# Level rows of the first batch picked on TensorE, and a state product with unequal weight widths, in a GateLoop and PReLU kernel

## The chip, the cores and the metric

The kernel runs on one core of one Trainium2 chip. It is one launch, and the time is that of the whole launch on the device in microseconds (us), inputs read from HBM and the output written to HBM. Below, PE is TensorE, DVE is VectorE, ACT is ScalarE, POOL is GpSimd, and SP is SyncE, whose queue issues every DMA of this kernel.

## The reference

Two blocks follow each other, all in float32. The first is a recurrence with a complex, data-dependent gate (4 batches, 8 heads, 768 tokens, head dimension 48):

```
mag = sqrt(a_re^2 + a_im^2);  scale = min(mag, 0.999) / (mag + 1e-6)
a = (a_re + i a_im) * scale
for t:  S = a[:, :, t, :, None] * S + k[t] v[t]^T      # S is complex, 48 x 48 per head
        y[t] = q[t] @ real(S)
```

Its output, as 3072 rows of 384, goes through the second block:

```
h = x @ w_in                                  # 3072 x 2048
g = max(h, 0) + alpha * min(h, 0)
out = g @ w_out                               # 3072 x 384
```

## The kernel before

**Units.** The tokens of a batch are cut into 6 chunks of 128, so there are 24 units u = 6b + c, and six of them make the first batch. Real and imaginary parts lie on neighbouring partitions: 96 partitions are 48 dimensions times two. `gates` makes the decays and phases of up to three chunks at a time with DVE and ACT and sends them through HBM; `loads` brings q, k, phases (`PP`) and decays (`T`) of a unit back in.

**Inside a unit** (function `unit`). Each half of 64 tokens is split in six levels h = 1, 2, 4, 8, 16, 32: at level h, a run of h keys meets the run of h queries after it. DVE brings keys and queries to a common point (L579, L581, L637), ACT copies them together (L660, L676), PE multiplies them (`ps_lv`, L596), and DVE or ACT masks the result into `A` (L620, L610). The output of the level then needs the rows of v that belong to the level's keys, in their order, on partitions 0 to 63 of each half: that is the tile `VL`, six levels wide, and the matmuls are those of L760 into `ps_y`.

**The rows of v.** `loads_v` loads the chunk of v as it is (`V`, L523 to L528) and `VL` besides. For h = 1, 2 and 32, `VL` comes straight from HBM in ten DMAs a unit (L547); for h = 4, 8 and 16 `half_rows` first copies the rows of a whole batch from HBM to HBM in the wanted order (`vsc`, six DMAs a batch, L480), and two DMAs a unit fetch them (L551). `V` and `VL` each have one buffer.

**The state.** Keys are transposed on PE (`ps_kt`, L708), and ACT copies the result into `T`: 96 columns at L710, and once more the first 32 of them into columns 96 to 127 at L711, to fill the weights up. The state products (`ps_kv`, L720) are, for each of 8 heads, a first half and a second half of 64 weight columns, for one or two halves of tokens: 32 matmuls of 64 rows by 64 weight columns with 48 moving columns (16 in the last chunk of a batch, which needs one half only). DVE adds them to the state (L728, L731), and L746 multiplies state and queries into `ps_y`. ACT copies `ps_y` out (L771) and it goes to HBM as the next block's input.

**The second block.** 256 tokens make an m. `features` and `two_features` compute h (`ps_h`, L817 and L839) and the gate; `outputs` computes the first 512 rows with plain products (`ps_o`, L867), and from then on `seven` makes four half-size blocks of the output from seven products (L957). The weights come in eight pieces of each matrix and are put together from halves of 64-bit words by ACT and DVE (`to_f32`, L435 to L445) into `w_in_sb` and `w_out_sb`.

**The order.** Every function above is a generator, one per stream of work, and the string `ORDER` says whose turn it is: each letter runs one generator to its next `yield`, which issues a few instructions. Engines run their own queue in that order and wait for each other by semaphores; the numbers in the `yield`s are not read when the kernel is built. Letters A to I are the gates, J the loads, K `half_rows`, L `loads_v`, M to O the weights, P to Z and a to m the 24 units, n the loads of x, o the second block.

A float32 matmul of the program is two matmul instructions on PE, each with its own load of weights, so the profile counts twice as many as the code. The shape of PE's array that a matmul asks for follows from its rows and weight columns: 128x32 at L596, 128x64 at L746, 64x64 at L720 and L760, 128x128 for the second block.

Of the kernel before, what the change touches and what calls it, by code (L numbers as in the profile page):

```python
# [30 lines left out]
    "ABMABAAABABAAAAAAABMAAAAAMAAAABABBBJMMNMAAAJABBAAKAAAKJJAAAAAAAABBBABJABBBBBBNMBNPBBBPNPJBJKJKJBJBBB"  # L31
    "PNBBBPBBBBBBBBBPPPOOOOJLJCPJJLLKKCPOJLLLMLLLLLLLMLLJJOPOPOPNOPPPPONNPPQCPPPQNQCCCCPPPPPPPPPPQQPQPCNC"
    "CCPPPPPPPPPCQQNCCCCCONCCCQOQCNPCPQQQOJMMJPPLMLLJCNQQNORCJLnLCMLLJJJLCCCLLLLQCQRCRQQCCOQNQQQoooooooLL"
    "LNQQRRQNooQQCCCCCNCooQoOoQRQoCQORCCNRRoNooooooORoQOMJONQQoooooRNNOOQQQQRQQROQOQDQQJLRLLnLJJORoLLoooo"
    "LLDMLRNNoLLLLLLooooJDooDDRoooSoSoRRRRRRRRooooooooDRRoRRoRooooRNNNRDSDoDRoDRDSOooooooooRoDoDRSSRJJJJR"
    "RSNSSRRRRDoooooDSDTOooODSLRRoSSoLMLLMJLJLLLLLooSoDSoOTSNoooooSNoOooSSoSoSNSSSSoSDooToSoSooSTSNoooOOo"
    "oNMLLLLLTTSoTSTDSOoTTSDoooooDoDSOKTNoNNNOSSSTSSTSJJJMJLSDDoooooSoooooDJLSSLoOToNTToooToOoOOoooooTTOT"
    "TToTDDTToooooUTnTTooLLLJJLJLDLLLUooooTDToDDoooLLLoLKDoJJJToTTUooDDoDDDTDJTDDDoooooUoTTUTUTTUUUUoVooo"
    "oooooUoTUUVUTTTTVooooooooUUUEJJLLLJJELLLLLLLLLJoLLooooVoEooooUUoUUUEoEVooooooEoEoUVUoUUUoooooUooooEU"
    "UVVUUVUVVVEEEooooooooVoUoKEUVKVUUUUJKKEUUUUKJJJVEVVooVooooEoooEEooEooVVVooooVVVVVVoWoWooooooVoVooJLL"  # L40
    "LJnWooVooVWoLLLLVWWEVEVEEEWEVWWLLLLLLLLEVWWVJEJoKJoooooooooooVVVWVWVVVELKVVLLLLJLJJLLLJJWoWWEWoooooo"
    "oooXXooEEEoEEoooooooooooooooooWWWWWWWoooWXoEWLLLoEoooooooooooWWooooWWoooXoXWWEEEWEEWoJLLLJoooWXWWWEW"
    "XWWWXYWXLWWLLFYXJLnLJJLoooooooXooooooooooooooXXXXXXoooooFoooooooXXFXXoXXXoXooooooooXoXoXYYooooLLLLLL"
    "LLooXXYYXooXYXYYLYooooXooooXFYFooooooXXXXYXYXFYoFYXXXLXLJLJJJLJLLLFooooooooYYoJooooooooooFoooooYYYFF"
    "YooYYooYYoJJLLLJLLJLoZoYooZooYooooFFoooFoYooYYFZoooFFLLooooooooooZooooZZYZYZYFZZYFYFYoooFZYYYZYZYYFo"
    "YooFFYooooooooooFFLLYJJJLooZooooooZZoooooooooooLnFLLFLJLLLJFooLJLLLLZaaFooooooZZoooZFaoFFZZoooooooaF"
    "FoZZZoZFFFoooooooZoooZooaaoooZoZoZZaaZFFFooFJJaoaaZooooooooooooZZZaZZZaZZaoooooooZaoaooabooooooooooo"
    "oooaaooabbZLLZLGJJLLJLJLLGLLLLLaaaoaaooaGooaoooooooJoboaoooaGoobGabaaaJJabbaLKKKoGbGoooooooooooobbbo"
    "ooGGooooGGooooboooooooooababaaGbaGGbGabaLaooooooooocoobLLJJGnKLoooooooooLoLLooobbooocbLLLLLJbbGGGoob"
    "ocooooooLLLKboboboooGGoboooocboooooobbccboocbGbGooooooocccGGoobboooobbbbooooooooooooGcGGKJGGGobcbcbo"  # L50
    "ocbJLJbbLLLJJLocccoooooooooooGooooccGcccocccGdGcoooooooooooocococoocooccoooGGGGcJLLLLLLLLLLdGcocGcoo"
    "oooooodoodooocccddcJJJcdcooooooooooooooooddLLccLHLcJJJLLLJLLdoLdHLLnoooooooodKLLLdddoddooooooooooooo"
    "ooddodddddooHeddoooeodooooodedoHdoooooooooooededdddeeoHddHooooooooeHeeoooHoooddoooooooooooooooddoeee"
    "oddoKJJJJddLLLJeJLLLJJJJLLLeoeoooooooooeHooooHooooooooooffHHooooeeeLJJLLLLLooooooHHHHHHHfooeeooeeeeo"
    "oooooeeoooooooooeoeoooeeeoeHHHfoHeHgefeoooooeeefeHeeKHooofofeeoJJHffoooooooonofHLJLLLLLLLHHooooooooo"
    "offfgoLLJLJJJLLLoofffooooooogHoLooooffoofHHfooooHHHoooooooooofffffoofoofoogoHooooHooooffooooofHHfffH"
    "ffHohhogooooooffgffgffofofhfgogooooooooooooooooggIJJLLLLLLLLJJJIJJgLLLLLLggIgoggIooooooIooooooooooog"
    "goghgIoggogoghIoogooooooogooIoogoogoghhgIhgghIhgoIooohhoooooooooioooooooohogIoIoghggghghhgIggLLLLJJn"
    "hhoooooooooooiLLLLLJLLLLLLJJooohhIhIhhIoooohhhIIihooooooooihoooooooooooooiIhooooooooooooooooooohhJoo"
    "oiiiihhohihIIIohihoooooooJhhihhihihLoohIIiooooooooooiihooooooooooooooiioihILLLoooIiiiijJJLLLJJLLLJji"  # L60
    "iJLLLLLIoiooiooiIiooioiIjiioIIIIIoIooooooooooIIIoiIoooooojiijijiijJIojjjjoooooooooooooooooooijjjjiio"
    "oiijJnJJJLLLLJLLojooooooooooooooooojjjjjjjkkjooooooooojjooojookooooooojoojoookookjkoooookkoooooooooo"
    "oojJJLLLLLLLLLjjoooooookoooooooooojookoooooookooojjjjkjkjjjkLjjkooooooooolkkoLLJJJJJooooookkkokkkook"
    "kooookokkooooolloookooklkllkkkkkloooollooooooooooolJLLLLLLLLLLJLLooooooooooloooooooooklkklkkkklkkLLL"
    "LLnlllooLLLJJLLooooooooooooooollolllloolllooooooolooolmmolloLLLLLoooooloooololmmlooooooooooolooooooo"
    "olmlmlmomomooooooooomoooooooooomoooolmlmlmooooomLLLLLLmomoooooooooLLLLoooooommoooommllmmmmmllLLLLooo"
    "oommoooooomooomooommmmmmmmmomooooooooooommmoooooooooooonoooooooooooooooooooooooooooooooooooooooooooo"
    "oooooooooooooooooooooooooooooooooooooooooooooooooooooooooooooooooooooooooooooooooooooooooooooooooooo"
    "oooooooooooooooooooooooooooooooooooooooooooooooooooooooooooooooooooooooooooooooooooooooooooooooo")
# [28 lines left out]
def kernel(  # L98
# [99 lines left out]
    def step(*args, **kwargs):  # L198
# [5 lines left out]
        KQ=3, PP=1, T=2, V=1, WQ=2, W=1, St=3, xT=2, raw0=1, raw1=1, raw2=1, raw3=1, g0=6, g1=6, g2=6, ot=2, top=2,  # L204
# [245 lines left out]
    def piece(dst, *key):  # L450
        if words:
            return (yield from to_f32(dst, *key))
        t = yield ACT(2 * DM, ("raw", *key))
        nc.scalar.copy(dst, raws[key])
        del raws[key]
        raw_done(*key, t)
        return t
# [10 lines left out]
    def half_rows():  # L468

        one = NCH * D2  # L470
        for b in range(B):
# [44 lines left out]

    def loads_v():
        for u in range(NU):
            b, c = divmod(u, NCH)
            yield DMA(172, ("KQ", u), takes=(R["V"],))  # L520
            L = loaded[u]
            L["V"] = V = work.tile([P, HP, D2], F32, tag="V", name="V", bufs=1)
# [31 lines left out]
            L["Vp"] = {name: VL[:, i] for i, name in enumerate(LEVELS)}  # L554
# [8 lines left out]
    def unit(u):  # L563
# [140 lines left out]
        for i in range(2):  # L704
            e = yield PE(0.333, k_, takes=(R["misc"],), n=2)
            t = ps.tile([P, HP, D2], F32, tag="misc", name="ps_kt")
            for p in range(4):
                nc.tensor.transpose(t[:, p], KQ[:, 1, 4 * i + p], ident[:D2, :D2])  # L708
            e = yield ACT(HP * P + 80, e, ("decays", u))
            nc.scalar.copy(T[:, 4 * i:4 * (i + 1), 0:D2], t)  # L710
            nc.scalar.copy(T[:, 4 * i:4 * (i + 1), D2:P], t[:, :, 0:P - D2])  # L711
            R["misc"].put(e)
# [3 lines left out]
        for n in range(H):  # L716
            for j in range(0, P, HC):
                for s in range(1 if last else 2):
                    rows = slice(HC * s, HC * (s + 1))
                    nc.tensor.matmul(kv[s][j:j + HC, n], lhsT=T[rows, n, j:j + HC],  # L720
# [422 lines left out]
```

## Time and profile before

| | |
|---|---|
| time, three runs | 762.88 us median (760.21 to 762.91) |
| the profiled execution | 765.08 us, of which the span of instructions is 763.4 us |
| PE busy | 674.9 us, 11728 matmul instructions |
| DVE busy | 605.4 us |
| ACT busy | 487.6 us |
| DMA | 130.61 MB, mean 171 GB/s |
| TensorE clock granted | full in nearly the whole span |

The busy share is told by stretch below. A matmul instruction is counted as busy from its start to the end of its way through the array, so neighbours overlap: a PE that is 100% busy may still have room between the starts of its matmuls. In timelines the first column is the start, and the distance from start to start is what a group of matmuls costs; the second column, its length, includes the way of the last one through the array.

### The profile page before, as it was taken

Reading aid. Unit: us, or ns where it says so; the run is one execution under the profiler, and the core shown is the slowest. Engines: PE = TensorE matmul, PEld = TensorE weight load, DVE = VectorE, ACT = ScalarE, POOL = GpSimd, SP = SyncE. Lnnn points to the kernel's source line nnn. Section 1 sums busy time; section 2 is a strip of 40 time slices with the busy share of each in tenths; the row PEclk is TensorE's granted clock in tenths of the full one; section 3 lists DMA queues with packets and bytes.
Section 4 is the critical chain, followed back from the end, with each engine's and each line's share of the span. In section 5 each row is a group of like instructions: output and inputs, shape, how many; then the busy total and the mean of one; then the engine's idle time right before and its main releaser. Section 6 shows DMA issues by size and latency. Waiting matters only on the chain.

```text
span 763.4 us, 26774 instructions
## 1 busy us (share of the span) xinstructions
PE 674.9 (88%) x11728; PEld 581.2 (76%) x11728; DVE 605.4 (79%) x798; ACT 487.6 (64%) x886; POOL 13.1 (2%) x48
## 2 busy tenths in 40 slices
PE   0024578999999999999999999999999999999998
PEld 0024456776767888888888889888888988889987
DVE  7889889998999799898986898888996765742323
ACT  8868888985658576946693666756584544453330
POOL 5000000000000000000000000000000000000000
PEclk9999999999999999999999999999999999999999
DMA  9999989979677936787668854865745743421000
GB/s 257 273 258 230 267 236 274 232 216 245 192 194 201 254 83 140 210 223 187 177 170 210 234 123 102 227 188 135 185 129 171 183 104 81 112 43 53 1 21 21
DMA packets 177180, 130.61 MB, mean 171 GB/s; under 512 B 66280, under 2 KB 168424, under 8 KB 176616
## 3 DMA queue, kind: packets, MB, share of 16 engines
q1 hardware_dynamic: 177064, 128.91, 64.3%
q8 instruction: 92, 1.51, 0.9%
q14 instruction: 24, 0.20, 0.1%
HBM read 100.52 MB, written 35.42 MB: 178 GB/s over the span
## 4 chain that ended last, share of the span: by engine, by line
PE 53%; DMA 16%; DVE 11%; SPq 6%; ACT 4%; issue 2%; DVEq 0%; ACTq 0%
PE ps_h L839 19%; PE ps_o L957 17%; PE ps_lv L596 4%; PE ps_y L760 3%; DVE KQ L637 3%; DMA PP<-phs 3%; PE ps_o L867 3%; DMA T<-decs 2%; PE ps_kv L720 2%; SPq L547 2%; PE ps_y L746 2%; DMA xT<-ysc 2%; DMA shared<-in_w_out_dram 2%; DMA VL<-vsc 2%; PE ps_h L817 1%
## 5 line engine op out<-in xcount | busy, mean ns | idle before, releaser
L839 PE MATMUL ps_h<-xT,w_in_sb 128*128 128x256 f32 x960 | 228.6, 384 | 0.7 <-DVE shared L854 0.6
L839 PEld LDWEIGHTS ps_h<-xT,w_in_sb 128*128 128x128 f32 x960 | 176.9, 190 | 22.6 <-DVE shared L854 0.8
L637 DVE TENSOR_TENSOR KQ<-KQ,T 96x1024 f32<-96x1024 f32 x120 | 145.8, 1215 | 28.6 <-PE ps_lv L596 18.9
L957 PE MATMUL ps_o<-w_out_sb,shared 128*128 128x192 f32 x624 | 111.4, 329 | 0.8 <-ACT top L973 0.4
L854 DVE TENSOR_TENSOR shared<-shared,ps_h 128x512 f32<-128x512 f32 x80 | 54.5, 682 | 68.2 <-ACT shared L852 67.9
L957 PEld LDWEIGHTS ps_o<-w_out_sb,shared 128*128 128x128 f32 x624 | 102.4, 190 | 3.5 <-DVE top L963 0.8
L848 ACT ACTIVATE shared<-ps_h 128x512 f32<-128x512 f32 x80 | 47.7, 596 | 80.6 <-PE ps_h L839 80.2
L957 PE MATMUL ps_o<-shared 128*128 128x192 f32 x448 | 80.3, 331 | 0.7 <-DVE top L963 0.7
L852 ACT ACTIVATE shared<-shared,al 128x256 f32<-128x256 f32 x160 | 74.5, 505 | 1.9
L957 PEld LDWEIGHTS ps_o<-shared 128*128 128x128 f32 x448 | 72.7, 190 | 3.3 <-DVE top L963 1.4
L660 ACT COPY WQ<-KQ 96x1024 f32<-96x1024 f32 x48 | 49.9, 1039 | 33.9 <-DVE KQ L637 33.7
L596 PE MATMUL ps_lv<-WQ 96*32 96x32 f32 x2304 | 34.4, 203 | 38.2 <-DVE WQ L579 26.0
L596 PEld LDWEIGHTS ps_lv<-WQ 96*32 96x32 f32 x2304 | 26.2, 116 | 52.4 <-DVE WQ L579 26.0
L817 PE MATMUL ps_h<-xT,w_in_sb 128*128 128x256 f32 (+1 forms) x240 | 53.3, 357 | 4.5 <-DMA xT<-ysc 4.5
L867 PE MATMUL ps_o<-w_out_sb,shared 128*128 128x384 f32 x128 | 51.3, 509 | 5.6 <-DVE shared L826 4.2
L817 PEld LDWEIGHTS ps_h<-xT,w_in_sb 128*128 128x128 f32 x240 | 41.9, 203 | 16.4 <-DMA xT<-ysc 5.2
L760 PE MATMUL ps_y<-A,VL 64*48 64x64 f32 x2304 | 49.1, 225 | 4.5 <-DMA VL<-vsc 4.4
L610 ACT ACTIVATE A<-ps_lv,columns 128x64 f32<-128x64 f32 x144 | 38.3, 334 | 21.4 <-PE ps_lv L596 21.0
L771 ACT COPY T<-ps_y 48x512 f32<-48x512 f32 x48 | 27.7, 576 | 34.5 <-PE ps_y L760 33.7
L676 ACT COPY W<-KQ 96x512 f32<-96x512 f32 x48 | 30.6, 637 | 29.5 <-DVE KQ L637 29.5
L760 PEld LDWEIGHTS ps_y<-A,VL 64*48 64x48 f32 x2304 | 39.4, 123 | 11.0 <-DMA VL<-vsc 5.8
L596 PE MATMUL ps_lv<-KQ,W 96*32 96x32 f32 x1536 | 23.4, 203 | 15.9 <-ACT W L676 15.8
(108 smaller groups left out, 955.8 us busy)
## 6 DMA issues: line engine op xcount, KB each, us to landing
T<-decs SPq DMA_DIRECT2D x48, 384.0 KB
PP<-phs SPq DMA_DIRECT2D x24, 387.0 KB
KQ<-in_q_dram SPq DMA_DIRECT2D x48, 192.0 KB
phs<-gate SPq DMA_DIRECT2D x14, 577.5 KB
decs<-gate SPq DMA_DIRECT2D x7, 1152.0 KB
KQ<-in_k_dram SPq DMA_DIRECT2D x40, 192.0 KB
vsc<-in_v_dram SPq DMA_DIRECT2D x24, 288.0 KB
VL<-vsc SPq DMA_DIRECT2D x48, 144.0 KB
```

The source lines that it names most:

```text
L596: nc.tensor.matmul(t[64 * i + j:64 * i + j + HC // 2, p], lhsT=keys(n, g), rhs=queries(n, g), start=True, stop=True)
L610: nc.scalar.activation(a[:, :, cols], t[:, :, at:at + name], AF.Copy, scale=s)
L637: nc.vector.tensor_tensor(out=x, in0=x if x0 is None else x0, in1=m, op=ALU.mult)
L660: nc.scalar.copy(z.rearrange("p i n t -> p i (n t)").rearrange("p i (m h) -> p m i h", h=h), bass.AP(tensor=KQ.tensor, offset=KQ.offset + ...
L760: nc.tensor.matmul(o, lhsT=Vp[h][64 * i:64 * i + 64, s, e_ * D:(e_ + 1) * D], rhs=a, start=False, stop=(s == 1 and h == LEVELS[-1]))
L817: nc.tensor.matmul(p, lhsT=w_in_sb[:, f // 2, kk, f % 2 * P:(f % 2 + 1) * P], rhs=x_of[m][:, kk, c * P:(c + n) * P], start=(kk == 0), stop ...
L839: nc.tensor.matmul(p[:, i], lhsT=w_in_sb[:, f // 2, kk, i * P:(i + 1) * P], rhs=x_of[m][:, kk], start=(kk == 0), stop=(kk == NK - 1))
L848: nc.scalar.activation(gt, p, AF.Relu, scale=-1.0)
L852: nc.scalar.activation(some_, some_, AF.Copy, scale=al_1[:, f + i:f + i + 1])
L854: nc.vector.tensor_tensor(out=gt, in0=gt, in1=p, op=ALU.add)
L867: nc.tensor.matmul(sums[0], lhsT=gt, rhs=w_out_sb[:, f], start=(f == start), stop=(f == stop))
L957: nc.tensor.matmul(z, lhsT=a[:, i], rhs=w[:, i], start=i == 0, stop=i == F2 - 1)
```

## The change

1. In the first batch, `VL` isn't loaded any more. A new generator `picks` (letter p) makes it on PE: a matrix of zeros and ones per level (`pick`, cut out of the identity by six copies on POOL) times `V` gives the rows of the level. For each of the six units these are 12 matmuls of 128 rows by 64 weight columns with 192 moving columns, four to a PSUM buffer of the ring `lv`, and three copies by ACT of 128x384 from PSUM to `VL`. The 12 `VL` DMAs of each of these units and the six `vsc` DMAs of the batch are gone. The other three batches do as before.
2. `V` has a second buffer for the even units of the first batch. It lies in the place of row block 14 of `w_out_sb`, and the picking matrices lie in that of row block 15, so the last piece of `w_out` is put together only after the last pick and after unit 4.
3. The second half of the state product has 32 weight columns in place of 64, in every unit: 64 and 32 columns make the 96 rows of the state. ACT's second copy (L711) is gone. The number of matmuls stays.
4. `ORDER` is another string altogether, found anew with longer transfers assumed.

The diff without the strings of the order:

```
-        KQ=3, PP=1, T=2, V=1, WQ=2, W=1, St=3, xT=2, raw0=1, raw1=1, raw2=1, raw3=1, g0=6, g1=6, g2=6, ot=2, top=2,
+        KQ=3, PP=1, T=2, V=1, Va=1, VL=1, WQ=2, W=1, St=3, xT=2, raw0=1, raw1=1, raw2=1, raw3=1, g0=6, g1=6, g2=6, ot=2, top=2,
...
     def to_f32(dst, *key):
         n = 2 * DM
-        ta = yield ACT(n + 100, ("raw", *key), takes=(R["top"],))
+        picked = [("picked", 0), ("V free", NCH - 2)] * (key == ("out", NF // 2 - 1))
+        ta = yield ACT(n + 100, ("raw", *key), *picked, takes=(R["top"],))
...
     def half_rows():
-        for b in range(B):
+        for b in range(1, B):
...
+    def v_ring(u):
+        return "Va" if u < NCH and u % 2 == 0 else "V"
+
     def loads_v():
         for u in range(NU):
             b, c = divmod(u, NCH)
-            yield DMA(172, ("KQ", u), takes=(R["V"],))
+            yield DMA(172, ("KQ", u), takes=(R[v_ring(u)],))
             L = loaded[u]
-            L["V"] = V = work.tile([P, HP, D2], F32, tag="V", name="V", bufs=1)
+            if v_ring(u) == "V":
+                V = work.tile([P, HP, D2], F32, tag="V", name="V", bufs=1)
+            else:
+                V = w_out_sb[:, NF - 2].rearrange("p (n e) -> p n e", n=HP)
+            L["V"] = V
...
             done["values", u] = t_
-            yield DMA(98)
+            if not b:
+                done["VL", u] = t_
+                continue
+            yield DMA(98, takes=(R["VL"],))
...
             del vsc_of[u]
-            L["Vp"] = {name: VL[:, i] for i, name in enumerate(LEVELS)}
+            done["V", u] = t
...
+    pick = w_out_sb[:, NF - 1].rearrange("p (l t) -> p l t", l=len(LEVELS))
+    for k, h in enumerate(LEVELS):
+        nc.gpsimd.tensor_copy(pick[:, k].rearrange("p (m h) -> p m h", h=h), halves(ident, h)[:, :, 0])
+
+    def picks():
+        for u in range(NCH):
+            n = P - (u + 1 == NCH)
+            for at in range(0, len(LEVELS), 2):
+                e = yield PE(0.7, ("VL", u), takes=(R["lv"],), mode=2, n=4)
+                L = loaded[u]
+                p = ps.tile([P, 2, 2, D2], F32, tag="lv", name="ps_vl", bufs=2)
+                for k in range(2):
+                    for i in range(2):
+                        nc.tensor.matmul(p[HC * i:HC * (i + 1), k], lhsT=pick[0:n, at + k], rhs=L["V"][0:n, 2 * i:2 * i + 2],
+                                         start=True, stop=True)
+                if u + 1 == NCH and at + 2 == len(LEVELS):
+                    done["picked", 0] = e
+                t = yield ACT(4 * D2, e, takes=() if at else (R["VL"],))
+                if not at:
+                    VL = work.tile([P, len(LEVELS), 2, D2], F32, tag="VL", name="VL", bufs=1)
+                    L["Vp"] = {name: VL[:, i] for i, name in enumerate(LEVELS)}
+                nc.scalar.copy(VL[:, at:at + 2], p)
+                R["lv"].put(t)
             done["V", u] = t
...
             nc.scalar.copy(T[:, 4 * i:4 * (i + 1), 0:D2], t)
-            nc.scalar.copy(T[:, 4 * i:4 * (i + 1), D2:P], t[:, :, 0:P - D2])
             R["misc"].put(e)
...
         for n in range(H):
-            for j in range(0, P, HC):
+            for cols in (slice(0, HC), slice(HC, D2)):
                 for s in range(1 if last else 2):
                     rows = slice(HC * s, HC * (s + 1))
-                    nc.tensor.matmul(kv[s][j:j + HC, n], lhsT=T[rows, n, j:j + HC],
+                    nc.tensor.matmul(kv[s][cols, n], lhsT=T[rows, n, cols],
                                      rhs=V[rows, n // 2, (n % 2) * D:(n % 2 + 1) * D], start=True, stop=True)
...
-        for name in ("V", 1, 4, 16, 32):
+        for name in (v_ring(u), "VL", 1, 4, 16, 32):
             R[name].put(e)
+        done["V free", u] = e
...
+        plan.add(picks())
         plan.run(ORDER)
```

More of the change, by code (lines that the diff above doesn't have):

```diff
@@ L36 @@
[L36 to L50, printed above, removed]
```

66 lines of the change are left out of this document (41 added, 25 removed).

## The prediction

> **What bounds the kernel.** I read the busy time by stretches first, then PE's timeline, then the waits and the chain. Stretches (start and end, length, then busy time and instructions of PE, PE's weight loads, DVE, ACT, POOL, then clock, DMA share, GB/s):
>
> ```profile
> 80.00:100.00 20.00, 14.84 (x387) 12.41 (x378) 17.02 (x29) 17.96 (x32) 0.00 (x0) 1.00 1.01 273
> 160.00:180.00 20.00, 20.00 (x381) 15.08 (x380) 17.07 (x28) 12.36 (x23) 0.00 (x0) 1.00 0.89 244
> 200.00:240.00 40.00, 39.04 (x725) 28.64 (x722) 38.12 (x44) 27.73 (x47) 0.11 (x1) 1.00 0.73 194
> 280.00:320.00 40.00, 40.00 (x624) 35.88 (x623) 37.39 (x45) 30.05 (x51) 0.11 (x1) 1.00 0.67 166
> 500.00:550.00 50.00, 49.43 (x860) 44.10 (x854) 42.18 (x50) 33.29 (x66) 0.14 (x2) 1.00 0.63 161
> ```
>
> Up to about 140 us DMA (0.9 to 1.0) and DVE share the limit and PE has gaps (77 us up to 140). From there PE is full: between 240 and 700 us its stretches leave 4.6 us idle in all. PE runs in order, so after 220 us whatever lengthens its row of matmuls lengthens the kernel.
>
> The second view is PE's timeline late in the kernel, where nothing is waited for. The distance from start to start is the cost:
>
> ```profile
> 640.40 0.46 PE L596 MATMUL ps_lv<-WQ 96*32 96x32 f32 x32
> 640.79 0.93 PE L760 MATMUL ps_y<-A,VL 64*48 64x64 f32 x48
> ...
> 647.81 0.46 PE L596 MATMUL ps_lv<-WQ 96*32 96x32 f32 x32
> 648.08 0.49 PE L596 MATMUL ps_lv<-KQ 96*32 96x32 f32 x32
> 648.50 0.70 PE L839 MATMUL ps_h<-xT,w_in_sb 128*128 128x256 f32 x2
> ...
> 655.13 1.15 PE L720 MATMUL ps_kv<-V,T 64*64 64x48 f32 x64
> 656.21 0.70 PE L839 MATMUL ps_h<-xT,w_in_sb 128*128 128x256 f32 x2
> ...
> 662.03 0.65 PE L746 MATMUL ps_y<-KQ,St 96*48 96x64 f32 x16
> 662.61 0.46 PE L596 MATMUL ps_lv<-WQ 96*32 96x32 f32 x32
> ...
> 686.46 1.14 PE L720 MATMUL ps_kv<-V,T 64*64 64x48 f32 x32
> 687.52 1.38 PE L746 MATMUL ps_y<-KQ,St 96*48 96x64 f32 x32
> ```
>
> Two things are to be seen. First, a change of array shape costs time: 32 matmuls of L596 take 0.27 us when the same shape follows (647.81 to 648.08), 0.39 and 0.42 when another follows (640.40, 648.08). So a change is worth 0.12 to 0.15 us; I take 0.13. It is paid where only the width changes too: from L746 (128x64) to L596 (128x32), 16 matmuls take 0.58 us, eight rounds of two side by side at 0.056 and one change. Second, matmuls on separate parts of the array run side by side, and time goes by rounds: L720 takes 1.08 us for 64 matmuls and 1.06 for 32 (last chunk of a batch, half of the rows). That is 16 rounds of 0.059 and one change. A round of 32 weight columns is 0.27 / 8 = 0.034.
>
> **The change part by part.** I sum against the profiled execution, 765.1 us (span 763.4 and 1.7 around it), 2.2 above the median of 762.9.
>
> *State products, all 24 units.* The order of matmuls is now, per head, 64 wide for one or two token halves, then 32 wide, and so on: shapes 64x64 and 64x32 alternate 15 times in a unit. In the two programs' orders I count 288 changes of shape before and 681 after, 360 of them inside state products. A head then costs two rounds of 64 (0.118), a change (0.13), two rounds of 32 (0.068), a change (0.13): 0.446 us, 3.57 a unit against 1.08, so +2.5. Lower end: the widths still share their rounds and only changes are paid at the cheapest, 15 x 0.12 = 1.8. If a change between these two isn't one, zero (first rival). The value taken is nearest to the rows of L746 and L596, which differ in width alone. In the timeline 17 units have their product after 220 us: 42.5, of which 3 go into PE's 4.6 us idle: +39.5. Four units lie between 140 and 220 (10 us, 3 in gaps): +7. Three lie before 120 us, in PE's gaps: +1; without that cover 7.5. Sum +47.5.
>
> [...]
>
> *First batch's DMAs.* Gone are 6 x 576 KB of `VL` (eight of 24 KB, two of 48, two of 144) and 6 x 288 KB of `vsc`, 5.2 MB. At the 253 to 279 GB/s of the first 100 us that is 20 us of all DMA engines, and 78 of 700 issues on SP, which took about 0.6 us each. The chain shows where that tells: DMA and SP carry most of it between 74 and 126 us (w_in, w_out, phases, decays, gates, and ten issues in SP's queue), and pieces at 167 to 178 and 204 to 214.
>
> ```profile
> PE 53%; DMA 16%; DVE 11%; SPq 6%; ACT 4%; issue 2%; DVEq 0%; ACTq 0%
> ```
>
> What comes after is DVE, whose idle time between 20 and 240 us is 18.4 us in all, and DVE has as much work for the first batch as before. So at most 18 us, at least none; I take -10, about the middle, since the chain between 126 and 165 us is DVE and PE already. V's second buffer belongs here: its load waits no longer for the last matmul of the unit before.
>
> *Picks.* 72 matmuls, 144 instructions of 192 columns. L957 has that width: 16 in 2.60 us, 0.163 each. Two column halves side by side, as in L746, give 72 x 0.163 = 11.7 us; one after the other 23.4. Units 0 to 3 lie where PE has gaps; units 4 and 5 (24 matmuls, 3.9 us) don't: +4. Ends: 0 and 23. Outside the state products, changes of shape grow by 40 in the first batch (13 of them in units 4 and 5, 1.7 us) and fall by 7 later (0.9): +1.
>
> *ACT.* L711 is gone:
>
> ```profile
> L711 ACT COPY T<-ps_kt 128x128 f32<-128x128 f32 x48 | 13.4, 279 | 0.0
> ```
>
> ACT isn't the limit; what counts is that PE's weight loads waited for it 7.5 us at L708 and 3.3 at L720, 6.7 of that before 220 us. I take -2, ends -10.8 and 0. The 18 copies of picks are nearest to L710 (128x384 from PSUM, 0.479): 8.6 us, less 12 x 0.279 in the same batch, +5 us of ACT. ACT's gaps up to 240 us hide it (12.4 of 20 busy at 160); without them +5.
>
> *New waits, costed at nothing.* The first copy of a unit's picks waits on ACT until `VL` is free, that is for the last L760 of the unit before; behind it stand masks, gates and weights. ACT waits for the same event to copy `ps_y` (L771), so it waits once. The last piece of `w_out` waits for the last pick; behind it stand two ACT steps of 1.0 and 1.1 us and one of DVE of 0.95, and the 23rd `ps_o` group of 384 columns follows closely: up to 3 us of PE if the cover, two groups of the second block, isn't there. Six POOL copies (0.32 each for the nearest, 64x64) come ahead of the masks, while PE's first matmul waits until 26 us.
>
> Sum: 47.5 - 10 + 4 + 1 - 2 = +40.5. The profiled execution would be 806 us, the median 803.
>
> **The rivals.**
>
> *The two widths don't count as a change* (20%). All changes of shape in the trace go between parts of the array that overlap; 64 columns at 0 and 32 columns at 64 don't. If PE runs them side by side as before, the state products cost nothing and the rest, -10 + 4 + 1 - 2 = -7, makes it faster: 756 us. For it: narrow weights are quick (a round of 0.034 against 0.059). Against it: L746 to L596 pays though only the width differs. It decides below 7 us / (21 units without cover x 15) = 0.022 us a change, a sixth of the cheapest row.
>
> [...]
>
> *Only the changes are paid, at the low end* (17%): 1.8 a unit, 21 x 1.8 = 38, less 6 in gaps, -7: +25, 788 us.
>
> *The early stage gives nothing back* (6%): PE meets picks in its queue whose `V` hasn't landed, holds the level products behind them, and no relief comes. Then 47.5 + 20 for picks: +68, 831 us.
>
> *The relief isn't there, since DVE bounds the first batch*: +50, 813 us; I count it into my forecast.
>
> **How the numbers follow.** My case has 57%, by itself 792 to 816 us. With the rivals at 20, 17 and 6%, the range of 8 in 10 takes in the low-end case and most of the first rival, whose own spread is about 748 to 766: 753 to 819. What a measurement of this kernel can tell from no change is about 0.5%, 3.8 us. Faster by more: 0.16, nearly all of the first rival; within: 0.04; slower: 0.80.
>
> **What would show it.** In the timeline after, a state product should take 3 to 4 us from start to start in place of 1.08, in eight pairs of 64 and 32 columns; 1.1 us would make the forecast wrong. PE's stretches past 240 us should be as full as before with fewer matmuls in them, and the weight loads' busy share lower. The first batch should show DMA below 0.9, `ps_y` of unit 2 out earlier than 124 us, and 18 copies to `VL`. If the last `ps_y` comes later by 35 to 45 us and the stretch after it is unchanged, the step is right; if the loss lies before 200 us, the picks or the order did it.

## The result, and the profile after

| | before | after |
|---|---|---|
| time, three runs | 762.88 us median (760.21 to 762.91) | 841.93 us median (832.48 to 842.16) |
| ratio | | 1.101, 95% interval 1.089 to 1.113 |
| profiled execution, its span | 765.08, 763.4 us | 842.16, 840.5 us |
| PE busy | 674.9 us | 773.0 us |
| `ps_y` of unit 2, 5, 7 and 23 copied out (second of the unit's two copies), against before | | 9, 17, 34 and 77 us later |

It is slower by 79 us. The forecast was slower by 40, with 819 us as the upper end: the direction and the main cause held, the size did not.

The page of the changed kernel: busy time, PE's granted clock and DMA over 40 slices of 21 us, and the shares of the chain that ended last.

```profile
PE 773.0 (92%) x11872; PEld 649.2 (77%) x11872; DVE 607.4 (72%) x798; ACT 487.6 (58%) x855; POOL 14.8 (2%) x54
...
PEclk9996698999998999999999998998999999999999
DMA  9896796559538446567466754755544735411000
...
PE 82%; ACT 7%; DVE 5%; DMA 4%; issue 2%; SPq 0%; DVEq 0%; ACTq 0%
```

DMA has nearly left the chain (16% before, 4% now) and SP's queue with it (6%, 0%), as the change meant. PE took all of that and more: 53% became 82%. The clock, full in the kernel before from 133 us on, falls again and again, late in the kernel too. The first 100 us of a clock row say little. The trace of the kernel before has no clock record before 88.6 us, that of the changed kernel none before 63.9 us, and a row shows full there; yet in the kernel before a state product took 1.98 us at 57.31, where later ones take 1.08.

By stretches (start and end, length, then busy time and instructions of PE, its weight loads, DVE, ACT, POOL, then clock, DMA share, GB/s):

```profile
80.00:100.00 20.00, 16.29 (x224) 12.15 (x228) 16.54 (x27) 16.13 (x25) 0.11 (x1) 0.55 0.70 210
160.00:180.00 20.00, 19.16 (x370) 13.77 (x373) 16.14 (x22) 15.39 (x27) 0.11 (x1) 1.00 0.69 190
200.00:240.00 40.00, 40.00 (x599) 29.98 (x597) 32.25 (x39) 20.77 (x37) 0.11 (x1) 0.96 0.66 188
280.00:320.00 40.00, 39.77 (x701) 33.59 (x703) 32.63 (x37) 26.84 (x49) 0.11 (x1) 1.00 0.38 99
500.00:550.00 50.00, 50.00 (x748) 42.96 (x747) 38.55 (x47) 32.40 (x58) 0.11 (x1) 0.90 0.62 158
```

The last row has 748 matmul instructions in 50 us of full PE, where the kernel before had 860. DMA's share in the first batch is 0.70 and 0.69 in place of 1.01 and 0.89, and yet PE and DVE get no further for it: DVE is busy 16.5 of 20 us at 80, where it was 17.0, and 32.3 of 40 at 200, where it was 38.1.

PE's timeline around one state product (start, length, then what):

```profile
604.27 0.46 PE L635 MATMUL ps_lv<-WQ 96*32 96x32 f32 x32
604.66 3.73 PE L758 MATMUL ps_kv<-V,T 64*64 64x48 f32 x64
608.33 0.46 PE L635 MATMUL ps_lv<-KQ,W 96*32 96x32 f32 x32
```

From start to start the product takes 3.67 us (most of them 3.63); the forecast was 3.57, and before it was 1.08. What a change of shape adds, 0.126 us by the experiments below, is called a drain from here on. What the forecast did not have comes right behind such a product:

```profile
265.03 3.70 PE L758 MATMUL ps_kv<-V,T 64*64 64x48 f32 x64
268.66 0.65 PE L635 MATMUL ps_lv<-WQ 96*32 96x32 f32 x32
269.10 0.65 PE L635 MATMUL ps_lv<-KQ,W 96*32 96x32 f32 x32
269.68 1.95 PE L784 MATMUL ps_y<-KQ,St 96*48 96x64 f32 x32
271.55 8.70 PE L878 MATMUL ps_h<-xT,w_in_sb 128*128 128x256 f32 x30
```

and the same place by stretches of 5 us:

```profile
265.00:270.00 5.00, 5.00 (x135) 3.96 (x136) 0.86 (x3) 0.48 (x2) 0.00 (x0) 0.87 0.91 318
270.00:275.00 5.00, 5.00 (x40) 4.23 (x37) 3.84 (x5) 1.52 (x2) 0.00 (x0) 0.50 0.85 214
275.00:280.00 5.00, 5.00 (x23) 4.18 (x22) 3.16 (x5) 2.53 (x6) 0.00 (x0) 0.95 0.75 252
```

After the product the clock is 0.50 for 6.8 us, and dense work (matmuls that follow each other without a change of shape) takes twice its time there. L784 takes 1.95 us where it took 1.10 at 614.75. The thirty matmuls of L878 take 8.70 us, where thirty of the same take 6.70 in the first experiment below: their first 3.95 us lie in the piece of half clock and do the work of 1.97. After 240 us the trace's clock records show half clock in pieces of 3.4 or 6.8 us (330.15 to 333.56, 268.71 to 275.54). In its profiled execution the kernel before has none there that PE works in; the changed kernel has 37.5 us of PE's work in eight pieces, so about 19 us are lost.

### The profile page after: what moved, and what is told of

It is laid out like the page before. It is cut to its first block, busy times and chain, and to the rows that moved or that the text cites. A ratio compares the mean times of both kernels' runs of the same rounds, so it can differ in the third digit from the quotient of the medians.

```text
span 840.5 us, 26948 instructions
## 1 busy us (share of the span) xinstructions
PE 773.0 (92%) x11872; PEld 649.2 (77%) x11872; DVE 607.4 (72%) x798; ACT 487.6 (58%) x855; POOL 14.8 (2%) x54
## 4 chain that ended last, share of the span: by engine, by line
PE 82%; ACT 7%; DVE 5%; DMA 4%; issue 2%; SPq 0%; DVEq 0%; ACTq 0%
PE ps_h L878 24%; PE ps_o L996 21%; PE ps_kv L758 11%; PE ps_lv L635 6%; PE ps_o L906 5%; PE ps_h L856 4%; PE ps_y L798 4%; PE ps_y L784 3%; PE ps_kt L747 2%; DVE KQ L676 1%; DMA gate<-in_a_re_dram 1%; DMA T<-decs 1%; PE ps_h L996 1%; PE ps_vl L584 1%; DVE gate L358 1%
## 5 line engine op out<-in xcount | busy, mean ns | idle before, releaser
L878 PE MATMUL ps_h<-xT,w_in_sb 128*128 128x256 f32 x960 | 231.5, 389 | 0.2 <-DVE shared L893 0.2
L878 PEld LDWEIGHTS ps_h<-xT,w_in_sb 128*128 128x128 f32 x960 | 182.7, 195 | 23.7 <-DVE shared L893 0.6
L996 PE MATMUL ps_o<-w_out_sb,shared 128*128 128x192 f32 x624 | 113.2, 332 | 0.4 <-ACT top L1012 0.4
L996 PE MATMUL ps_o<-shared 128*128 128x192 f32 x448 | 87.1, 347 | 0.0
L758 PE MATMUL ps_kv<-V,T 64*64 64x48 f32 (+1 forms) x1216 | 80.3, 230 | 0.0
L996 PEld LDWEIGHTS ps_o<-shared 128*128 128x128 f32 x448 | 78.7, 202 | 2.0 <-DVE top L1023 0.2
L758 PEld LDWEIGHTS ps_kv<-V,T 64*64 64x64 f32 (+1 forms) x1216 | 57.7, 121 | 23.9 <-issue 2.1
L906 PE MATMUL ps_o<-w_out_sb,shared 128*128 128x384 f32 x128 | 52.7, 521 | 2.4 <-DVE shared L865 2.3
L856 PEld LDWEIGHTS ps_h<-xT,w_in_sb 128*128 128x128 f32 x240 | 42.3, 203 | 12.6 <-issue 0.9
L769 DVE TENSOR_TENSOR St<-St,ps_kv 96x384 f32<-96x384 f32 x44 | 24.1, 548 | 33.6 <-PE ps_kv L758 32.6
L635 PEld LDWEIGHTS ps_lv<-WQ 96*32 96x32 f32 x2304 | 26.9, 117 | 27.5 <-ACT VL L592 11.1
L635 PE MATMUL ps_lv<-WQ 96*32 96x32 f32 x2304 | 35.2, 205 | 12.2 <-ACT VL L592 9.5
```

The lines of the kernel that those rows point to most:

```text
L635: nc.tensor.matmul(t[64 * i + j:64 * i + j + HC // 2, p], lhsT=keys(n, g), rhs=queries(n, g), start=True, stop=True)
L758: nc.tensor.matmul(kv[s][cols, n], lhsT=T[rows, n, cols], rhs=V[rows, n // 2, (n % 2) * D:(n % 2 + 1) * D], start=True, stop=True)
L856: nc.tensor.matmul(p, lhsT=w_in_sb[:, f // 2, kk, f % 2 * P:(f % 2 + 1) * P], rhs=x_of[m][:, kk, c * P:(c + n) * P], start=(kk == 0), stop ...
L878: nc.tensor.matmul(p[:, i], lhsT=w_in_sb[:, f // 2, kk, i * P:(i + 1) * P], rhs=x_of[m][:, kk], start=(kk == 0), stop=(kk == NK - 1))
L906: nc.tensor.matmul(sums[0], lhsT=gt, rhs=w_out_sb[:, f], start=(f == start), stop=(f == stop))
L996: nc.tensor.matmul(z, lhsT=a[:, i], rhs=w[:, i], start=i == 0, stop=i == F2 - 1)
```

## Experiments

The ratios are to the kernel before, run on the same chip at the same time; its median there was 764 to 770 us.

### The state product alone, with the rest kept, and the rest without it

The first takes the unequal widths out of the changed kernel: two halves of 64 again, with the second ACT copy that they need.

```
+            nc.scalar.copy(T[:, 4 * i:4 * (i + 1), D2:P], t[:, :, 0:P - D2])
...
-            for cols in (slice(0, HC), slice(HC, D2)):
+            for cols in (slice(0, HC), slice(HC, P)):
```

> The changed kernel with the second half of the state product 64 weight columns wide again, and ACT's second copy back; picks, V's second buffer and the new order stay. Theory A (the loss is the 15 changes of array shape in each state product, and the clock that falls because of them): a product back at 1.1 us, granted clock 0.99 or more, time 755 to 772 us. Rival B (a good part of the loss is picks and order in the first batch, since the sixth unit's output came 17 us late): 778 us or more. If the relief of DMA that I forecast exists, below 763.

Measured: 772.73 us, 1.0101 (1.0053 to 1.0149), just above the first theory's range. A product is back at 1.08 us:

```profile
615.00 1.15 PE L759 MATMUL ps_kv<-V,T 64*64 64x48 f32 x64
616.08 0.46 PE L635 MATMUL ps_lv<-WQ 96*32 96x32 f32 x32
```

and the thirty matmuls at full clock, from this run's chain, are

```profile
251.22 6.70 PE ps_h L879 x30
```

So the widths carry 1.101 - 1.010 = 0.091 of the loss, 69 us; and what is left of the change, forecast to gain 5 us with the ACT copy kept, still costs 1%.

The second puts the widths alone into the kernel before:

```
-            nc.scalar.copy(T[:, 4 * i:4 * (i + 1), D2:P], t[:, :, 0:P - D2])
...
-            for j in range(0, P, HC):
+            for cols in (slice(0, HC), slice(HC, D2)):
```

> The kernel before with the 32-column second half of the state product alone (and without ACT's second copy); order, loads and buffers as before. Theory A: a product of 3.7 us, 24 x 2.6 = 62 us more on PE, less what the first units' gaps hide (about 10), plus 10 to 20 us of clock: 815 to 840 us, granted clock 0.94 to 0.98. Rival B: at most 805.

Measured: 830.42 us, 1.0853 (1.0786 to 1.0921), 65 us. The product is as in the changed kernel, in the old order with its old transfers:

```profile
683.51 3.70 PE L719 MATMUL ps_kv<-V,T 64*64 64x48 f32 x64
687.14 0.46 PE L596 MATMUL ps_lv<-WQ 96*32 96x32 f32 x32
```

It has 30.7 us of PE's work at half clock after 240 us. The two runs agree: the widths cost 65 to 69 us wherever they stand.

### How many changes of shape: the drain, and the clock behind it

The same matmuls with the same widths, in another order: all 64-wide ones of a product first, then all 32-wide ones, so one change of shape inside it in place of 15.

```
-        for n in range(H):
-            for cols in (slice(0, HC), slice(HC, D2)):
+        for cols in (slice(0, HC), slice(HC, D2)):
+            for n in range(H):
```

> The changed kernel with the state product's matmuls in another sequence: all 64-column ones first, then all 32-column ones; the same matmuls, one change of shape inside a product in place of 15. Theory A: 16 rounds of 0.059 and 16 of 0.034 and two changes, 1.75 us a product, 0.65 more than at 64 columns: 14 to 16 us above the run with 64 columns, 770 to 788 us, clock 0.99 or more. Rival C (the 64x32 shape is slow by itself, whatever stands beside it): a product above 3 us and 825 us or more.

Measured: 784.34 us, 1.0244 (1.0194 to 1.0295). The product takes 1.87 us:

```profile
647.64 1.94 PE L758 MATMUL ps_kv<-V,T 64*64 64x48 f32 x64
649.51 0.46 PE L635 MATMUL ps_lv<-WQ 96*32 96x32 f32 x32
```

Then heads 0 to 3 alternate and 4 to 7 are grouped, 9 changes inside a product; two more runs let five and six heads alternate, 11 and 13 changes.

```
-        for n in range(H):
-            for cols in (slice(0, HC), slice(HC, D2)):
+        low, high = slice(0, HC), slice(HC, D2)
+        for n, cols in ([(n, cols) for n in range(H // 2) for cols in (low, high)]
+                        + [(n, cols) for cols in (low, high) for n in range(H // 2, H)]):
...
```

> The changed kernel with heads 0 to 3 alternating as in the change and heads 4 to 7 grouped (four of 64 columns, then four of 32): 8 to 9 changes of shape inside a product in place of 15. Theory A: a product of 2.7 us, 1.6 more than at 64 columns, 36 to 39 us above the run with 64 columns. If the clock only falls when a thin stretch fills a whole window of about 3.4 us, it stays at 0.99 and the time is 793 to 808; if it falls in proportion to the changes, 0.965 to 0.975 and 803 to 820.

> The changed kernel with heads 0 to 4 of a state product alternating between 64 and 32 columns and heads 5 to 7 grouped: 11 changes of shape inside a product, against 15 in the changed kernel, 9 with four heads alternating (1.0553 of the kernel before, product 2.88 us from start to start) and 1 with all heads grouped (1.0244, 1.87 us). Nothing else differs. By the row of those two, 0.126 us a change, the product takes 3.13 us. Without half clock behind the products: 1.0553 + 2 x 0.126 x 21 / 764 = 1.062 of the kernel before, 811 us, on the straight line of the two. With it: 8 to 20 us above that line, 1.072 to 1.088.

> The changed kernel with heads 0 to 5 alternating and heads 6 and 7 grouped: 13 changes of shape inside a product, 3.38 us by 0.126 a change. Theory A (half clock is a cost of its own, about 20 us in the changed kernel, set off when the thin stretch fills a piece of 3.4 us): just under the bound, no half clock after 220 us and 1.0553 + 4 x 0.126 x 21 / 764 = 1.069, 817 us; the last two changes, to the changed kernel, then cost some 25 us, of which 5 are the drains. Rival (no cost of its own; the loss goes up smoothly with the changes): half clock or not, the time lies on a curve between 1.0553 at 9 and 1.101 at 15 changes, 1.082 to 1.088 here, 827 to 831 us.

Measured, with the products and PE's work at half clock after 240 us (most products, and the shortest and longest):

| changes inside a product | product, start to start | ratio to before | PE's work at half clock after 240 us |
|---|---|---|---|
| 0 (all 64 wide) | 1.08 us (1.06 to 1.20) | 1.0101 (1.0053 to 1.0149) | 0 |
| 1 | 1.87 us (1.85 to 1.89) | 1.0244 (1.0194 to 1.0295) | 0 |
| 9 | 2.88 us (2.81 to 2.90) | 1.0553 (1.0489 to 1.0616) | 0 |
| 11 | 3.13 us (3.05 to 3.31) | 1.0607 (1.0567 to 1.0648) | 10.2 us |
| 13 | 3.38 us (3.29 to 3.77) | 1.0716 (1.0675 to 1.0758) | 10.2 us |
| 15 (the changed kernel) | 3.63 us (3.53 to 4.13) | 1.101 (1.089 to 1.113) | 37.5 us |

With four heads alternating, a product looks like this, with no half clock behind it:

```profile
644.44 2.94 PE L760 MATMUL ps_kv<-V,T 64*64 64x48 f32 x64
647.32 0.46 PE L635 MATMUL ps_lv<-WQ 96*32 96x32 f32 x32
```

Between 1 and 9 changes the product grows by (2.88 - 1.87) / 8 = 0.126 us a change, which is the 0.12 to 0.15 that the trace of before showed for other shapes, and it goes on at that price to 15. Up to 13 changes the time follows: 11 was expected at 1.062 and 13 at 1.069 on that line, and both intervals hold these values; the smooth curve's 1.082 to 1.088 for 13 is excluded. The last two changes cost 0.029, 22 us (10 us either way, as the changed kernel has three runs), of which 2 x 0.126 x 21 = 5.3 us are drains, while 27 us more of half clock, some 14 us lost, come with them. So the clock is a cost of its own, the 17 us (10 either way) that the drains leave.

Where the pieces stand tells more. At 11 and at 13 changes there are two after 240 us, each in or behind a product of a batch's last chunk, which has half the matmuls with the same changes of shape; behind the 14 full products, up to 3.42 us long, there is none. At 15 changes six of the 14 full products and two of the three of last chunks have one. So full products of 3.63 us show it, and those of up to 3.42 do not. That it was to be wholly absent at 13 changes was a miss.

Half clock shows without a long product too. In the run without the first batch's loads (below), whose products take 1.08 us, PE stands still for 1.71 us, and half clock follows:

```profile
518.82 0.45 PE L751 MATMUL ps_y<-KQ,St 96*48 96x64 f32 x4 [1.71 <-issue]
519.20 1.22 PE L844 MATMUL ps_h<-xT,w_in_sb 128*128 128x256 f32 x2
520.22 5.21 PE L962 MATMUL ps_o<-shared 128*128 128x192 f32 x16
```

The sixteen matmuls of the last row take 2.76 us at 509.15 in the same run. It has 6.4 us of PE's work at half clock after 240 us; the run without the second ACT copy has 6.8, behind standstills of 1.56 and 1.83 us. So the 10.2 us at 11 and 13 changes are little more than short products can have, and the 37.5 and 30.7 us at 15 changes are far more. Each of these figures is of one execution.

### Cutting the product in two

> The changed kernel with the state products of units 6 to 23 cut in two: heads 0 to 3, then (in 15 of the 18 units) the next two matmul steps of the MLP, 128x128 or 128 wide, drawn forward in the order, then heads 4 to 7. Every change of shape inside the product stays, one to three are added per unit; only the thin stretch of 3.7 us becomes two of about 1.9 us. Theory A (some 20 us of the loss are half clock, which a thin stretch of 3.7 us sets off and one of 2.95 us does not): no pieces of half clock after 220 us but perhaps behind the three uncut products, and 842 - 20 + 18 x 0.13 to 0.4 us = 824 to 829 us, 1.078 to 1.086 of the kernel before. Rival (the half clock is a mark of the drains and not a cost of its own): the time stays at 840 to 847 us, 1.10 to 1.11, or the half clock stays where it was.

```
         for n in range(H):
+            if n == H // 2 and u >= NCH:
+                e = yield PE(0.72, e, mode=2, n=32)
```

In the order, two matmul steps of the MLP stand between the halves. Measured: 842.70 us, 1.0988 (1.0950 to 1.1025): a miss, since nothing is gained; it is the time that the rival gave. A unit looks like this:

```profile
424.19 1.89 PE L760 MATMUL ps_kv<-V,T 64*64 64x48 f32 x32
426.01 0.92 PE L998 MATMUL ps_o<-w_out_sb,shared 128*128 128x192 f32 x4
426.86 1.89 PE L760 MATMUL ps_kv<-V,T 64*64 64x48 f32 x32
428.67 0.46 PE L635 MATMUL ps_lv<-KQ,W 96*32 96x32 f32 x32
```

The trace accounts for it. PE's work at half clock after 240 us fell from 37.5 to 17.1 us, not to none. One of the three pieces left comes behind a standstill of 2.18 us; the two others lie in products of last chunks, with 0.85 and 0.96 us of dense work between the halves. That gives back 10 us. PE's busy time there, 595.8 in the changed kernel and 591.4 here, is 577.0 and 582.9 us with the half clock taken out, so the cut itself added 6 us of drains and broken groups; and PE's idle time there grew from 5 to 10 us, 2.2 of it in one wait for the state. This run by itself neither shows nor refutes the clock's cost; the step from 13 to 15 changes shows it.

### One narrow shape throughout

If the change of shape is the price and not the narrow weights, three blocks of 32 columns should be quick. In the kernel before, without the second ACT copy:

```
-            for j in range(0, P, HC):
+            for j in range(0, D2, 32):
...
```

> The kernel before with the state products in three blocks of 32 weight columns (0, 32, 64) in place of two of 64: all matmuls of a product have one shape, 64x32, so there is no change of shape inside; the ACT copy L711 goes, since column 96 on is no longer read. Theory A (the price of the changed kernel is the change of shape, not the narrow weights): 16 rounds of 0.034 (six side by side as fast as four) to 0.051 (by the matmul) and one change, 0.67 to 0.95 us a product against 1.08; 21 products give -3 to -9 us, so 0.3 to 1.1% faster than the kernel before, and no half clock after a product. Rival (64-row, 32-column blocks drain whatever stands beside them): a product of 3 us or more, 800 us or more.

Measured: 784.36 us, 1.0246 (1.0204 to 1.0288). Whole products take 1.02 to 1.16 us (568.73 to 569.75 and 650.64 to 651.78 in the timeline), so 96 matmuls of one narrow shape cost about what 64 wide ones cost, more than the 0.67 to 0.95 us expected, and nothing like 3 us: the rival falls. But the kernel got slower by 19 us, which neither side expected. The timeline shows where:

```profile
621.17 0.91 PE L719 MATMUL ps_kv<-V,T 64*32 64x48 f32 x75
623.43 0.38 PE L719 MATMUL ps_kv<-V,T 64*32 64x48 f32 x21 [1.35 <-issue]
623.74 0.46 PE L596 MATMUL ps_lv<-KQ,W 96*32 96x32 f32 x32
```

In the middle of a product PE stands still for 1.35 us with nothing that it waits for. The view of waits after 240 us has more of them:

```profile
PE ps_y L745 <- issue: 5.2, 2, 2.7
PE ps_y L759 <- issue: 2.6, 3, 1.4
PE ps_lv L596 <- issue: 1.8, 2, 1.5
PE ps_kv L719 <- issue: 1.6, 2, 1.4
```

(us in total, times, longest). Over the span these are 23.8 us in 16 places; the kernel before has none. The program has 704 matmul instructions more, and the DMA queue that the profile lists as `instruction` moved 98 packets in place of 92. That the instructions come too late is a reading that fits, but it was argued from these rows and not tried by itself. The count alone does not explain it: the other variants, with as many matmul instructions as before or 144 more, have between 0 and 10.3 us of such standstills (10.3 in the changed kernel with 64-wide halves).

> The changed kernel (new order, picks, V in two buffers, no ACT copy) with the same three blocks of 32 columns in the state products, all of one shape. Theory A: the clock's share and the drains go together, and it lands 0 to 9 us under the changed kernel with 64-wide products (1.0101 of before): 0.999 to 1.010 of the kernel before, 763 to 773 us. Rival: as in the old order, 3 us a product or more, and above 820 us.

The same in the changed kernel: 801.28 us, 1.0449 (1.0401 to 1.0497), between what the two sides expected and a miss for both: against the changed kernel with 64-wide halves (1.0101) the narrow blocks cost 27 us. Undisturbed products take 1.02 us here too. In the profiled execution (810.21 us, the slowest of six) PE stands still with no wait shown for 25.0 us in 12 places after 240 us, up to 4.8 us at a time, and 26.4 us of its work there are at half clock, with no long product ahead of it.

### The first batch: relief, picks and order

The kernel before, without the first batch's loads of `VL` and `vsc`:

```
+            if not b:
+                nc.gpsimd.memset(VL, 0.0)
...
-                        nc.sync.dma_start(dst, src)
+                        if b:
+                            nc.sync.dma_start(dst, src)
...
```

> The kernel before, with the first batch's loads of VL and vsc left out (5.2 MB, 78 issues); VL is set to zero by POOL in each of these six units, so the level products of the first batch multiply zeros and that part of the output is not the reference's. No picks, the old order, old state products. It measures the relief by itself. Theory R (the term of the prediction, -10 with ends -18 and 0, is there, and something else in the change eats it): about 1.3% faster than the kernel before, 753 to 760 us beside 766. Theory D (DVE and ACT hold the first batch, and DMA waits are replaced by theirs): within 0.4% of the kernel before; DMA and SP leave the chain, and the share that they had goes to DVE and ACT.

Measured: 764.00 us, 0.9988 (0.9966 to 1.0010), 1 us. The relief that the forecast took at 10 us is worth 2.6 us at most.

The changed kernel with 64-wide halves, without the picks:

```
-                p = ps.tile([P, 2, 2, D2], F32, tag="lv", name="ps_vl", bufs=2)
-                for k in range(2):
-                    for i in range(2):
-                        nc.tensor.matmul(p[HC * i:HC * (i + 1), k], lhsT=pick[0:n, at + k], rhs=L["V"][0:n, 2 * i:2 * i + 2],
-                                         start=True, stop=True)
...
-                nc.scalar.copy(VL[:, at:at + 2], p)
+                if not at:
+                    nc.gpsimd.memset(VL, 0.0)
```

> The changed kernel with the state products 64 wide again and the ACT copy back, and with the picks and their 18 copies to VL left out (POOL sets VL to zero once a unit, so the level products of the first batch multiply zeros). New order, V in two buffers. Against the same kernel with picks (772.7 us, 1.0101 of before) it measures the picks. If the picks cost the loss: 1.0 to 2.0% faster than that, 757 to 765 us, level with the old order without loads. If the new order costs it: 768 to 773 us, and it stays about 1% above the old order without loads.

Measured: 772.43 us, 1.0113 (1.0079 to 1.0146), against 1.0101 with the picks. In this order the picks cost nothing that shows (-1 us, 4.5 us either way), and the loss stays when they go. This run and the run without loads do the same work on PE, DVE and ACT; they differ in the order and in `V`'s second buffer, and in 1.25% of time, 9.6 us (3 us either way). What PE and DVE had done between 20 and 240 us, and what was left, in the run without loads in the old order:

```profile
20.00:240.00 220.00, 161.56 (x3319) 123.14 (x3320) 205.90 (x271) 177.31 (x290) 8.63 (x15) 0.96 0.83 218
...
240.00:850.00 610.00, 513.84 (x8410) 458.61 (x8408) 386.56 (x496) 296.68 (x573) 1.07 (x11) 0.99 0.45 119
```

and in the new order without picks:

```profile
20.00:240.00 220.00, 161.16 (x3228) 122.01 (x3232) 197.30 (x258) 168.28 (x272) 7.05 (x15) 0.91 0.80 212
...
240.00:850.00 610.00, 521.33 (x8524) 465.33 (x8510) 394.66 (x504) 303.58 (x589) 1.06 (x11) 1.00 0.46 121
```

By 240 us DVE has done 8.6 us less in the new order, and PE has 7.5 us more left, which is about the difference of the spans (770.1 and 762.8 us). Of DVE's 8.6 us, 3.3 fall between 20 and 80 us, where one wait of 3.6 us is for PE's level products (`ps_lv`), 2.4 between 80 and 160 us and 2.9 after that. What DVE waits for between 160 and 240 us is, in the new order,

```profile
DVE shared L862 <- ACT shared L860: 5.4, 7, 1.9
DVE KQ L672 <- PE ps_lv L631: 1.7, 2, 1.4
```

and in the old one, for the same gate step of the MLP,

```profile
DVE shared L831 <- ACT shared L829: 0.8, 3, 0.4
```

So the waits that DVE has more of in the new order are for ACT and PE. It is not the half clock of the early stage, though the records show 28.5 us of PE's work at half clock before 240 us against 7.5. Most of the difference, 16.5 us, lies between 100 and 240 us, and there the run with the picks, in the same order and as late (1.0101), has none. Whether `V`'s second buffer or the order of the rest costs the 9.6 us was not taken apart.

The other way round, the picks in the old order: the letters of the loads are taken out, each unit's picks stand ahead of its transposes and its state product, and `V` has one buffer (for units 4 and 5 POOL makes the picking matrices once more in another place, as the last piece of `w_out` comes before them).

> The kernel before in its own order, with the first batch's level rows picked by TensorE: the loads of VL and vsc are taken out of the order, and each unit's three pairs of picks stand ahead of its two transposes of keys and its state product. V has one buffer, the state products are as before, 64 wide. All outputs are computed. Against the run with the new order and 64-wide products (1.0101 of before) it tells the order and V's second buffer from the picks. Theory R with costly order: 757 to 762 us (-10 for the relief, +4 for picks), 0.5 to 1.2% faster than before. Theory D with costly picks: 768 to 775 us, 0.3 to 1.2% slower, as in the new order, since 72 products (11.7 us of PE) and 18 copies (8.6 us of ACT) are added where nothing is given back.

Measured: 779.76 us, 1.0209 (1.0175 to 1.0244), 16 us, more than either side expected. From PE's waits between 20 and 240 us:

```profile
PE ps_vl L589 <- DMA V<-in_v_dram: 6.3, 2, 5.1
```

With one buffer, `V` arrives late and the picks stand waiting for it in PE's queue with the level products behind them. That accounts for 6.3 of the 16 us; the rest was not taken apart, and no other place for the picks in this order was tried. So the changed kernel's second buffer and new order together do serve the picks: 16 us become 8 (1.0101), but not a gain.

### The second ACT copy

In the kernel before, the copy L711 goes, and POOL fills the corner of `T` that it filled:

```
+                    nc.gpsimd.memset(T[D2:P, :, D2:P], 0.0)
...
-            nc.scalar.copy(T[:, 4 * i:4 * (i + 1), D2:P], t[:, :, 0:P - D2])
```

> The kernel before without the second ACT copy from the keys' transposes (48 of 0.279 us); POOL sets the 32 by 32 corner of T that it filled to zero once a unit, which reaches no result. It measures the term of -2 us (ends -10.8 and 0). Theory A (ACT is not the limit): -2, so 0 to 0.5% faster. Rival (PE's weight loads wait for ACT there, 7.5 and 3.3 us): 0.8 to 1.4% faster. A loss would mean that POOL's write holds up the transfers into T.

Measured: 764.34 us, 0.9999 (0.9978 to 1.0020). The copy is free. Of the 10.8 us that PE's weight loads waited for ACT at L708 and L720, 8.8 are still there, now for ACT's first copy (6.7 and 2.1).

No variant was faster than the kernel before.

## Why the prediction was wrong

The forecast was 803 us, the result 842. By its own steps, with 1% as 7.6 us:

| step | forecast | measured | by |
|---|---|---|---|
| state products, drains | +47.5 | +50 | line of 1 and 9 changes carried on to 15, 1.0553 + 6 x 0.126 x 21 / 764 = 1.076, less 1.0101 |
| half clock behind them | not in the sum | +19 | 1.101 less 1.076; and half of 37.5 us |
| first batch's DMAs | -10 | -1 | 0.9988 |
| new order and `V`'s buffer | +1, its changes of shape alone | +10 | 1.0113 less 0.9988 |
| picks | +4 | -1, so nothing | 1.0101 less 1.0113 |
| ACT copy | -2 | 0 | 0.9999 |
| sum | +40.5 | +77 | the medians differ by 79 |

The measured column is made of differences of the same ratios, so its sum is no test by itself. Two terms have a second source: half of 37.5 us, and (3.63 - 1.08) x 21 = 54 us for the drains.

*State products.* The step is right in mechanism, place and price: 3.57 us forecast and 3.63 to 3.67 measured, 0.13 us a change and 0.126 measured. The first rival, that two widths are no change, falls, and so does the low end of 1.8 us a unit. The row of 1 and 9 changes shows the price where only the width differs. The lower end of the first rival's spread, 748 us, was an estimate that no run shows: with one narrow shape throughout, a product took 1.02 to 1.16 us and the kernel 784. One part of the step was off: the cover in the early stage. By unit 2's output the changed kernel was 8 us behind its 64-wide twin (9.4 against 1.2 us later than before), where +1 was forecast. The first two products, at 52 and 89 us, took 5.44 us each in place of the twin's 1.89, and PE's gaps did not hide it. The records show half clock at the second (67.33 to 98.05 us) and nothing yet at the first, but behind it, at 57.55, L784 takes 1.95 us, as at half clock later (269.68).

*The clock* is the term that the sum lacked, half of the miss. I took a longer product to cost its own length; the step that failed is that what stands behind it would run as before. The profile calls PE busy all through it, and the kernel before, whose products take 1.08 us, shows the clock full from 133 us on; nothing in that trace could show from what length on, but it could have been named as a rival with a price. What the traces show is pieces of 3.4 and 6.8 us, in or behind eight of the 17 products after 240 us in the changed kernel, where the profile calls PE 100% busy, and behind standstills of 1.56 to 1.83 us in runs with short products. That a product sets one off by filling a piece of 3.4 us was the author's reading; it was not shown, and products of last chunks have pieces from 3.05 us on.

*The relief* failed at the step from "DMA and SP carry the chain between 74 and 126 us" to "-10, about the middle". I had bounded it by DVE's idle time, 18 us, and had named the case that DVE bounds the batch, worth 813. Without the loads, DMA falls from 16% to 7% of the chain and SP's queue from 6% to 1%, and DVE's busy time from 20 to 240 us rises only from 201.6 to 205.9 us. The units gain 4.7 us by unit 10, still 3.8 at unit 16 and 0.4 at the last; between units 16 and 17 lie the standstill and the half clock shown above, in this execution. So even at its largest the relief was half of the term.

*The order* failed as a step of its own: I counted its changes of shape (+1) and costed the rest at nothing, since no wait in it looked dear. An order found anew for other durations moves every engine's queue, and with `V`'s second buffer it came out 9.6 us dearer at equal work. Which of the two costs it stays open.

*Picks and ACT copy* were near enough: neither shows a cost. Four picks take 0.80 us where I had worked out 0.65 (143.66 to 144.46), and after the first, which is PE's first work at 25.8 us, none waits for `V`. A wait that I had not named is there: the level products stand 9.5 us, in two places, for ACT's copies to `VL` (L635 for L592); but the run without picks is no faster.

Of what the forecast said would be seen, the product, DMA below 0.9 and fewer matmuls in a full stretch (748 for 860 at 500 us) came true. `ps_y` of unit 2 came 9 us later, not earlier than 124 us, and the last one 77 us later, not 35 to 45.

## What to carry to other kernels

Keep the array's shape the same through a run of small matmuls, even at the price of wider weights: 25% fewer weight columns cost 50 us in drains here, and grouping by shape got back four fifths of the whole loss that they made. A long chain of drained matmuls can cost more than its length, here with half clock behind six of 14 full products of 3.63 us and behind none of 14 at up to 3.42, so look at the granted clock behind it. And before a transfer is bought off with work on another engine, leave the transfer out in one run: here that run showed at once that 5 MB less of DMA were worth 1 us.

## What was not expected of the hardware

- Half clock behind a PE that is shown as busy: after 240 us none behind full products of 1.08 to 3.42 us, six of 14 at 3.63 us, and at 11 and 13 changes four of the six products of last chunks, from 3.05 us on. In these pieces dense matmuls take double (L784 1.95 for 1.10 us).
- Half clock behind short standstills: 1.56, 1.71 and 1.83 us of idle PE each went with a piece of 3.4 or 6.8 us, in runs whose products take 1.08 us. The 1.35 us with three narrow blocks did not.
- In the first 100 us the clock rows can show full where matmuls run at half clock. At 13 changes the row from 0 to 100 us shows 1.00, at 11 changes 0.69, and yet the same two matmuls of L908 take 1.65 us in both (at 94.13 and 92.81 us), as they do in the changed kernel at 94.18 (L906), where its records show half clock.
- Narrow blocks with 704 more quick matmuls among 11728 (6%) came with 23.8 us of standstill on PE that no semaphore explains, up to 3.5 us at a time, where the kernel before has none; so a product that is as short as before can still make the kernel 2.5% slower. The cause was not isolated.
